# Linear attention into a two-expert router on one core: constants in pieces, gate sums moved, a new written-out order

## The chip, the core and the metric

One core of a Trainium2 chip runs the whole program. Its engines are TensorE (PE in the profile), VectorE (DVE), ScalarE (ACT), GpSimd (POOL) and SyncE (SP). Each has its own instruction queue and works through it in order; ACT, POOL and SP can also issue DMAs. The metric is the device time of one execution in microseconds (us), the median of several runs.

## The reference

```python
phi(x) = where(x > 0, x, exp(x) - 1) + 1              # on q and k
kv  = einsum('bhsd,bhse->bhde', phi(k), v);  z = sum(phi(k), axis=seq)
x   = (phi(q) @ kv) / (phi(q) . z + 1e-6)             # 8 batches, 8 heads, 576 rows of 64
x   = x as 4608 tokens of 512
noisy = x @ w_gate + log1p(exp(x @ w_noise)) * noise  # 8 experts
top2  = the two largest;  top2_w = exp(top2_l - max) / (sum + 1e-9)
out[token] = sum over its two experts e: top2_w * (relu(x @ w1[e]) @ w2[e])   # 512 -> 1024 -> 512
```

## The kernel before

**Attention.** Two batches form a group; there are four groups (0 to 3). q, k and v are loaded by POOL DMAs that turn fp32 into bf16. ACT takes the exponential of k and q (line 178), DVE makes phi of it (lines 187 and 190). PE multiplies k by v (line 210), transposes (229, 256) and makes numerators, denominators and router logits in one matmul group, `num` (line 272); DVE divides (287, 294).

**Routing.** A unit is a group, or the first six or last three of the nine column tiles of group 3 (units 3 and 4). `route(u)` is a generator of some 25 small DVE steps with a few on ACT and PE. It finds the two experts of each token (the lower-numbered is the first visit, the other the second) and each visit's rank in its expert's list. `dispatch` scatters 128 rows at a time from the tile `xr` into the DRAM table `x_sorted`, by indirect DMAs on POOL: 72 in all. A row is 512 bf16 values and four 4-byte fields (token, two gates, rank). In before.py the gates are normalised in `route` and the ranks are copied into a tile `posi`, from which the scatter takes its addresses.

**Experts.** `mm1` (line 669) and `mm2` (line 684) work on blocks of up to 512 rows. Blocks 0a, 0b, 1a, ... are named by expert; "0b" is the second block of expert 0. The first blocks hold first visits alone. A block in round 1 (0b, 1a, 2a) may be loaded when the first visits of units 0 and 1 are scattered, one in round 2 (0c, 1b, 2b, 3a) when those of unit 2 are too, and 0d when all five units are. `xt` is a transposed load, `xn` a plain one that PE transposes; both are issued on SP. Fields of a block are loaded apart, as `meta`. `mm2` also scales its result by the gate on DVE, and `put` writes it to `part` (first visits) or `out`.

**What sets the order.** Up to the end of the early blocks the order is written out by hand in `SCRIPT`: a list of words, each a call, which gives every engine its instructions in that order. `l` loads, `e`, `r`, `m` make phi, `K V T t U u Q q N n` are the attention, `R.u` is one step of `route(u)`, `D.u.s.c` scatters column tile c of unit u (s is 0 for first visits, 1 for second), `W.e.i` loads a weight matrix of expert e, `X`, `M`, `G`, `H`, `Y` are a block's load, fields, transposition, mm1 slice and mm2 tile. Behind SCRIPT, loops go over the remaining blocks (`PLAN`), unchanged here. Software DMAs of POOL use eight semaphores in turn, so that one waits until the eighth before it has landed.

Of the kernel before, what the change touches and what calls it, by code (L numbers as in the profile page):

```python
# [49 lines left out]
def build_constants(tc, consts, w_gate, w_noise, noise):  # L50
    nc = tc.nc
    c = {}
    tile_ = lambda name, shape, dt=FP32: consts.tile(shape, dt, name=name)


    wst = tile_("wst", [P, 4, 16])
    for half in range(2):
        for i, w in enumerate((w_gate, w_noise)):
            nc.scalar.dma_start(
                out=wst[64 * half : 64 * half + 64, :, 8 * i : 8 * i + 8],  # L60
                in_=w[256 * half : 256 * half + 256, :].rearrange("(a p) e -> p a e", p=64),
            )
    noise_sb = c["noise"] = tile_("noise_sb", [P, 4, 9, E])
    for g in range(4):
        nc.scalar.dma_start(
            out=noise_sb[:, g], in_=noise[g * 2 * S : (g + 1) * 2 * S, :].rearrange("(p c) e -> p c e", c=9))

    ident = c["ident"] = tile_("ident", [P, P], BF16)
    nc.gpsimd.memset(ident[:], 0.0)
    nc.gpsimd.affine_select(  # L70
        out=ident[:], in_=ident[:], compare_op=ALU.not_equal, fill=1.0,
        base=0, pattern=[[-1, P]], channel_multiplier=1,
    )
    c["gap"] = tile_("gap", [P, 8])
    ut = c["ut"] = tile_("ut", [P, P], BF16)
    nc.gpsimd.memset(ut[:], 0.0)
    nc.gpsimd.affine_select(
        out=ut[:], in_=ut[:], compare_op=ALU.is_ge, fill=1.0,
        base=0, pattern=[[-1, P]], channel_multiplier=1,
    )  # L80
    iota = lambda t, pattern, base, mult: nc.gpsimd.iota(
        t, pattern=pattern, base=base, channel_multiplier=mult, allow_small_or_imprecise_dtypes=True)

    tokid = c["tokid"] = tile_("tokid", [P, 9])
    iota(tokid[:], [[1, 9]], 0, 9)
    rowpos = c["rowpos"] = tile_("rowpos", [P, T_CAP])
    iota(rowpos[:], [[P, T_CAP]], 0, 1)

    c8 = c["c8"] = tile_("c8", [P, E])
    iota(c8[:], [[-1, E]], E, 0)  # L90
    nc.vector.tensor_scalar(out=c8[:], in0=c8[:], scalar1=1.0 / E, scalar2=None, op0=ALU.mult)

    ones = c["ones"] = tile_("ones", [P, P], BF16)
    nc.vector.memset(ones[:], 1.0)  # L94
    carry = c["carry"] = tile_("carry", [P, 2 * E])
    iota(carry[:], [[REGION, 2 * E]], 0, 0)
    c["bound"] = [tile_(f"bound{i}", [P, EARLY]) for i in range(len(ROUNDS))]
    for t, (_, q) in zip(c["bound"], ROUNDS):
        for e in range(EARLY):
            nc.vector.memset(t[:, e : e + 1], float(e * REGION + q[e]))  # L100
    rank0 = c["rank0"] = tile_("rank0", [P, 2 * E])
    iota(rank0[:], [[REGION, 2 * E]], 0, 0)

    c["f0"], c["s0"] = tile_("f0", [P, E]), tile_("s0", [P, E])
    for t, n, base in ((c["f0"], N_F, 0), (c["s0"], N_S, E * REGION)):
        step = n[1] - n[0]
        iota(t[:, 0:4], [[REGION + step * P, 4]], base + n[0] * P, 0)
        iota(t[:, 4:E], [[REGION + step * P, 4]], base + 4 * REGION + n[4] * P, 0)
    c["wst"], c["wblk"] = wst, tile_("wblk", [P, 4, 32], BF16)
    return c  # L110


class PhaseA:


    def __init__(self, rows, attn, rout, tc, q, k, v, x_sorted, psum):
# [14 lines left out]
        self.x, self.e, self.kvps, self.pqt, self.qtp, self.rden, self.r, self.ps, self.posi = {}, {}, {}, {}, {}, {}, {}, {}, {}  # L131

    def buffers(self):

        self.nc.vector.memset(self.v[:, 8:12, :], 1.0)
        self.xr = [self.pers.tile([P, 9, ROW_W], BF16, name=f"xr{i}") for i in range(3)]
        self.lwt = self.pers.tile([P, 9, 8, 16], FP32, name="lwt")
        self.kvbd = [self.kvp.tile([P, 2, 4, KVW], BF16, name=f"kvbd{i}") for i in range(2)]
        for t in self.kvbd:
            self.nc.vector.memset(t[0:64, :, :, 65:130], 0.0)  # L140
            self.nc.vector.memset(t[64:P, :, :, 0:65], 0.0)
        for t in self.xr:
            self.nc.vector.memset(t[:, :, HD:ROW_W], 0.0)
# [157 lines left out]
    def route(self, u):  # L301
# [72 lines left out]
        nc.vector.tensor_reduce(out=rank, in_=pr, op=ALU.add, axis=AX.X)  # L374
        yield
# [3 lines left out]
        yield  # L379
        nc.vector.scalar_tensor_tensor(out=gr, in0=ge[:, 0], scalar=1e-9, in1=ge[:, 1], op0=ALU.add, op1=ALU.add)  # L380
        yield
        nc.vector.reciprocal(out=gr, in_=gr)
        yield
        for i in range(2):
            tt(fld(1 + i), ge[:, i], gr, ALU.mult)
# [698 lines left out]
```

## Time and profile before

| | us |
|---|---|
| median of 3 runs (lowest to highest) | 415.59 (415.16 to 416.53) |
| the profiled execution | 419.67 |
| its span, first to last instruction | 417.9 |
| PE busy | 344.8 (83%) |
| POOL busy | 269.6 (65%) |
| ACT busy, DVE busy | 181.1, 178.1 |

The profile is of one execution, a little slower than the median. A busy PE is not a PE at its peak; what matters is where PE is idle, and what ends that. The page also gives the share of time in which the 16 DMA engines were busy; it can be over 1, since packets overlap.

### The profile page before, as it was taken

How to read it: one execution, taken by the hardware profiler on the slowest of the kernel's cores; microseconds unless marked ns; L12 is line 12 of the kernel's file. 1: busy time of each engine (PE TensorE's matmuls, PEld its weight loads, DVE VectorE, ACT ScalarE, POOL GpSimd, SP SyncE). 2: the span in 40 equal slices, each digit the busy share in tenths (PEclk: the TensorE clock that was granted, in tenths of full speed). 3: DMA queues.
4: the chain of work that ended last, by engine and by line, in shares of the span. 5: the costliest groups of instructions: out<-in, count | busy, mean ns of one | idle time of the engine just before them, and what ended most of it. 6: DMA issues, size and time to landing. Idle time of an engine off the chain costs nothing.

```text
span 417.9 us, 6947 instructions
## 1 busy us (share of the span) xinstructions
PE 344.8 (83%) x2519; PEld 205.5 (49%) x2549; DVE 178.1 (43%) x452; ACT 181.1 (43%) x342; POOL 269.6 (65%) x405
## 2 busy tenths in 40 slices
PE   0985666555751999989999999999999999999990
PEld 0354555444531665745556555644544544564440
DVE  0845979897770665113242324312421322332130
ACT  1569375754430443535444443443334334325410
POOL 8450158888768266875207576869849867898761
PEclk9996756888695899999999999999999999999997
DMA  8999999999999959998858999999997999954551
GB/s 123 205 207 207 234 199 220 216 196 174 208 215 194 244 175 271 228 252 271 149 164 180 181 243 212 205 261 192 303 249 161 245 145 312 214 181 130 172 200 57
DMA packets 83441, 85.59 MB, mean 205 GB/s; under 512 B 42911, under 2 KB 66146, under 8 KB 83398
## 3 DMA queue, kind: packets, MB, share of 16 engines
q0 software_dynamic: 36416, 63.92, 72.0%
q1 hardware_dynamic: 39222, 20.86, 23.1%
q10 hardware_dynamic: 7760, 0.28, 1.8%
q8 instruction: 22, 0.36, 0.3%
q14 instruction: 21, 0.17, 0.1%
HBM read 77.13 MB, written 33.79 MB: 265 GB/s over the span
## 4 chain that ended last, share of the span: by engine, by line
PE 66%; DMA 14%; POOL 7%; DVE 6%; issue 3%; ACT 3%; POOLq 0%; SPq 0%; DVEq 0%
PE b L669 29%; PE b L684 28%; DMA w<-in_moe_w_dram 6%; POOL x_sorted L412 4%; DMA xt<-x_sorted 3%; PE num L149 3%; DMA xn<-x_sorted 3%; DMA x_sorted<-xr,posi 2%; PE b L210 2%; DVE e L190 2%; PE num L272 2%; ACT e L178 2%; POOL kq L164 1%; DVE xr L287 1%; PE t L615 1%
## 5 line engine op out<-in xcount | busy, mean ns | idle before, releaser
L671 ACT ACTIVATE hT<-b 128x256 bf16<-128x256 f32 (+5 forms) x224 | 101.3, 460 | 153.9 <-PE b L669 147.6
L669 PE MATMUL b<-xt,w 128*128 128x256 bf16 (+5 forms) x890 | 149.0, 315 | 17.9 <-DMA xt<-x_sorted 16.7
L684 PE MATMUL b<-w,hT 128*128 128x512 bf16 (+1 forms) x616 | 141.9, 380 | 1.3
L669 PEld LDWEIGHTS <-w 128*128 128x128 bf16 x896 | 86.4, 99 | 72.4 <-issue 11.0
L412 POOL DMA_INDIRECT x_sorted<-xr,posi x72 | 75.9, 1054 | 30.9 <-issue 14.5
L684 PEld LDWEIGHTS <-hT 128*128 128x128 bf16 (+1 forms) x640 | 59.1, 99 | 63.2 <-issue 1.9
L178 ACT ACTIVATE e<-kq 128x2304 bf16<-128x2304 bf16 x16 | 33.4, 2127 | 23.3 <-DMA kq<-in_k_dram 12.8
L706 POOL DMA_INDIRECT out_dram<-y,si x34 | 33.7, 991 | 9.4 <-issue 5.5
L651 POOL DMA_INDIRECT L<-part,gi x34 | 34.8, 1023 | 7.7 <-issue 7.7
L651 POOL DMA_INDIRECT L<-part,mgi x12 | 12.0, 1003 | 37.9 <-issue 26.9
L272 PE MATMUL num<-kvbd,pqt 128*64 128x162 bf16 x288 | 18.4, 298 | 11.4 <-DVE xr L287 7.5
L287 DVE TENSOR_TENSOR xr<-num,rden 128x768 bf16<-128x768 f32 x24 | 22.7, 950 | 0.2
L272 PEld LDWEIGHTS <-pqt 128*64 128x64 bf16 x288 | 15.0, 145 | 14.5 <-DVE xr L287 8.4
L688 DVE SCALAR_TENSOR_TENSOR y<-b,mgate,L 128x512 f32<-128x512 f32 (+1 forms) x12 | 9.0, 746 | 30.8 <-PE b L684 23.9
L190 DVE TENSOR_TENSOR e<-e,kq 128x2304 bf16<-128x2304 bf16 x16 | 21.2, 1348 | 0.1
L149 PE MATMUL num<-ones 128*128 128x512 bf16 x44 | 12.2, 449 | 10.9 <-DVE ones L94 10.9
L210 PE MATMUL b<-v,e 64*128 64x192 bf16 x144 | 17.4, 289 | 2.8 <-DVE e L190 2.8
L164 POOL DMA_DIRECT2D v<-in_v_dram x20 | 13.6, 701 | 7.9 <-DMA kq<-in_q_dram 3.2
L164 POOL DMA_DIRECT2D kq<-in_k_dram x10 | 6.6, 694 | 17.3 <-DVE rden L281 12.4
L688 DVE SCALAR_TENSOR_TENSOR y<-b,meta7S,L 128x512 f32<-128x512 f32 (+1 forms) x10 | 7.5, 750 | 23.5 <-PE b L684 17.4
L210 PEld LDWEIGHTS <-e 64*128 64x128 bf16 x288 | 14.9, 113 | 5.1 <-DVE e L190 3.7
L210 PE MATMUL misc<-v,e 64*128 64x192 bf16 x144 | 17.4, 289 | 0.0
(165 smaller groups left out, 345.9 us busy)
## 6 DMA issues: line engine op xcount, KB each, us to landing
w<-in_moe_w_dram POOLq DMA_DIRECT2D x16, 1024.0 KB, 10.9
part<-y SPq DMA_DIRECT2D x39, 256.0 KB, 5.7
kq<-in_k_dram POOLq DMA_DIRECT2D x6, 576.0 KB, 9.8
kq<-in_q_dram POOLq DMA_DIRECT2D x6, 576.0 KB, 7.8
v<-in_v_dram POOLq DMA_DIRECT2D x12, 288.0 KB, 13.3
v<-in_v_dram POOLq DMA_DIRECT2D x8, 144.0 KB, 9.0
kq<-in_k_dram POOLq DMA_DIRECT2D x4, 288.0 KB, 7.5
kq<-in_q_dram POOLq DMA_DIRECT2D x4, 288.0 KB, 10.6
```

Of the source, the lines that this page charges most:

```text
L149: self.nc.tensor.matmul(out=ps[:, i % 4, 0:512], lhsT=self.c["ones"][:], rhs=_ap(self.c["ones"], [[0, 4], [1, P]]), start=True, stop=True)
L178: self.nc.scalar.activation(out=e, in_=x, func=ACT.Exp)
L190: nc.vector.tensor_tensor(out=e, in0=e, in1=x, op=ALU.min)
L210: nc.tensor.matmul(out=self.kvps[g, h, j][:, KVM * i : KVM * i + KVM], lhsT=e[half, hp, ci, :], rhs=v[half, hp + 8 - step : hp + 9 + step ...
L272: self.nc.tensor.matmul(out=ps[half, hp, KVW * i : KVW * i + KVW], lhsT=self.pqt[g, 3 * t + i][:, hp, half], rhs=self.kvbd[g % 2][:, j, hp ...
L287: nc.vector.tensor_tensor(out=_ap(xr, [[64, 4], [ROW_W, 3], [1, 64]], off=3 * t * ROW_W + 256 * s), in0=_ap(ps, [[512, 4], [KVW, 3], [1, 6 ...
L412: r = self.nc.gpsimd.indirect_dma_start(out=self.x_sorted, out_offset=bass.IndirectOffsetOnAxis(ap=self.posi[u][:, ci, sl : sl + 1], axis= ...
L651: r = nc.gpsimd.indirect_dma_start(out=L[0:m].bitcast(INT32), out_offset=None, in_=self.part.bitcast(INT32), in_offset=bass.IndirectOffset ...
L669: nc.tensor.matmul(out=ps[:, 0:n], lhsT=w1[:, dc, fc * P : fc * P + P], rhs=b["xt"][:, dc, 0:n], start=(dc == 0), stop=(dc == 3))
L671: nc.scalar.activation(out=b["hT"][:, fc, 0:n], in_=ps[:, 0:n], func=ACT.Relu)
L684: nc.tensor.matmul(out=ps[i * m : i * m + m], lhsT=b["hT"][:, f, t * P : t * P + m], rhs=w2[:, f, :], start=(fc == 0), stop=(fc == 8 // n ...
L706: r = nc.gpsimd.indirect_dma_start(out=self.out, out_offset=bass.IndirectOffsetOnAxis(ap=self.m[e, kind, i]["si"][0:m], axis=0), in_=y[0:m ...
```

## The change

Constants are built in pieces, as words of SCRIPT: `ones` and the warm-up matmuls (52 for 44) come first on DVE and PE, the router weights are loaded on SP and the noise on ACT between its exponentials (both were on ACT ahead of all else). Group 0 loads k, then v, then q (v came first). `route` writes exponentials and ranks straight into the scattered row; the scatter takes its addresses from there. The division by the gates' sum is done by `gates`, three DVE instructions for a `meta` tile before its first use. `mm2` is split: its evacuation and `put` are a word of their own, `y`. And SCRIPT is in a new order.

```diff
-        posi = self.posi[u] = self.rt.tile([P, 9, 2], INT32, name="posi", bufs=len(UNITS))
-        nc.vector.tensor_copy(out=_ap(posi, [[1, 2], [2, n]]), in_=rank)
-        nc.vector.tensor_copy(out=fld(3).bitcast(INT32), in_=rank[:, 0])
-        nc.vector.scalar_tensor_tensor(out=gr, in0=ge[:, 0], scalar=1e-9, in1=ge[:, 1], op0=ALU.add, op1=ALU.add)
-        nc.vector.reciprocal(out=gr, in_=gr)
-        for i in range(2):
-            tt(fld(1 + i), ge[:, i], gr, ALU.mult)
+        nc.vector.tensor_reduce(out=pair(3).bitcast(INT32), in_=pr, op=ALU.add, axis=AX.X)
...
-            out_offset=bass.IndirectOffsetOnAxis(ap=self.posi[u][:, ci, sl : sl + 1], axis=0),
+            out_offset=bass.IndirectOffsetOnAxis(ap=row[:, HD // 2 + 3 + sl : HD // 2 + 4 + sl], axis=0),
...
+    def gates(self, f):
+        nc, n = self.nc, f.shape[1]
+        d = self.mp.tile([P, T_CAP], FP32, name="gsum")[:, 0:n]
+        nc.vector.scalar_tensor_tensor(out=d, in0=f[:, :, 1], scalar=1e-9, in1=f[:, :, 2], op0=ALU.add, op1=ALU.add)
+        nc.vector.reciprocal(out=d, in_=d)
+        nc.vector.tensor_tensor(out=f[:, :, 1:3], in0=f[:, :, 1:3], in1=_ap(d, [[1, n], [0, 2]]), op=ALU.mult)
...
 SCRIPT = """
-l.v0.0 l.k0.0 l.k0.1 l.q0.0 l.q0.1 C l.v0.1 l.k1 e.k0.1 e.k0.0 r.k0.1 m.k0.1 r.k0.0 m.k0.0 l.q1 l.v1 e.q0.0 e.q0.1 wb
+l.k0.0 buf.1 c.ones warm.52 l.k0.1 buf.2 e.k0.0 l.v0.0 l.q0.1 c.squares l.q0.0 r.k0.0 c.counts l.v0.1 l.k1 c.router
```

Up to the last first visit of units 0 and 1, POOL has 29 scatters and four weight loads before, and 27 scatters and four weight loads now; W.1.0 has moved ahead of five scatters of unit 0, and W.2.0, which stood two places behind that last first visit, stands nine scatters behind it.

Three places show what moves. SP, from the zeros to the first results: `meta0F` and the first `xt` are of block 0a, the next `xt` of 0b, 1a and 2a. Before and after:

```order
L807 DMA part<-zrow 1x288
L466 DMA meta0F_914<-x_sorted 128x2x4
L589 DMA_TRANSPOSE xt<-x_sorted 128x4x256 x2
L589 DMA_TRANSPOSE xt<-x_sorted 128x4x384
L589 DMA_TRANSPOSE xt<-x_sorted 128x4x256
L466 DMA meta1F_1708<-x_sorted 128x3x4
```
```order
L836 DMA part<-zrow 1x288
L466 DMA meta0F_918<-x_sorted 128x2x4
L610 DMA_TRANSPOSE xt<-x_sorted 128x4x256
L466 DMA meta2F_1691<-x_sorted 128x2x4
L610 DMA_TRANSPOSE xt<-x_sorted 128x4x256
L610 DMA_TRANSPOSE xt<-x_sorted 128x4x384
```

The fields of 2a now stand ahead of the rows of 0b. PE, from the second `num` of group 3 (hT is 0a's, w_834 and w_839 are expert 0's w2, w_833 and w_838 its w1), before and after:

```order
L272 MATMUL num<-kvbd_187,pqt 64x162
L684 LDWEIGHTS hT
L684 MATMUL b<-w_834,hT 128x512
...
L669 LDWEIGHTS w_833
L669 MATMUL b<-xt,w_833 128x256
```
```order
L277 MATMUL num<-kvbd_115,pqt 64x162
L690 LDWEIGHTS w_838
L690 MATMUL b<-xt,w_838 128x256
...
L704 LDWEIGHTS hT
L704 MATMUL b<-w_839,hT 128x512
```

One slice of 0b (H.0b.7, which needs its `xt`) now stands ahead of the first mm2 tile of 0a (Y.0a.0). POOL, at the first scatter of unit 3 (xr_184 and xr_179 hold unit 2, xr_182 and xr_177 unit 3), before and after:

```order
L412 DMA x_sorted<-xr_184,posi 73984x288
L405 MEMSET gap 128x8
L412 DMA x_sorted<-xr_182,posi 73984x288
L405 MEMSET gap 128x8
L412 DMA x_sorted<-xr_184,posi 73984x288
```
```order
L412 DMA x_sorted<-xr_177 73984x288
L404 MEMSET gap 128x8
L412 DMA x_sorted<-xr_179 73984x288
L404 MEMSET gap 128x8
L412 DMA x_sorted<-xr_179 73984x288
L404 MEMSET gap 128x8
L412 DMA x_sorted<-xr_179 73984x288
```

Before, all first visits of unit 2 stand ahead of unit 3's first scatter (the one behind it is a second visit); now three of them (D.2.0.3, D.2.0.8, D.2.0.2) stand behind D.3.0.1.

## Rows read from the trace of the kernel before

**Rows 1.** Busy time by stage (counts in brackets), then granted clock, DMA share, GB/s

```profile
23.00:44.00 21.00, 13.81 (x201) 11.49 (x202) 12.23 (x17) 15.62 (x20) 5.30 (x9) 0.74 1.21 208
...
120.00:133.50 13.50, 2.82 (x31) 1.55 (x32) 5.53 (x16) 0.85 (x2) 11.55 (x21) 0.70 1.09 182
133.50:165.00 31.50, 30.80 (x206) 18.86 (x210) 19.37 (x79) 11.52 (x33) 16.52 (x30) 0.91 0.96 227
165.00:188.50 23.50, 21.30 (x160) 14.73 (x160) 3.00 (x4) 12.17 (x29) 18.50 (x34) 1.00 1.03 240
188.50:240.00 51.50, 51.18 (x333) 29.48 (x337) 17.71 (x60) 24.56 (x52) 20.70 (x30) 1.00 0.84 187
...
360.00:408.00 48.00, 47.20 (x257) 23.90 (x260) 14.62 (x22) 15.22 (x33) 37.86 (x45) 1.00 0.56 175
```

**Rows 2.** Chain that ended last, 113 to 190 us: start, us, what

```profile
113.83 6.61 DMA x_sorted<-xr,posi
120.46 13.03 DMA xt<-x_sorted
...
133.53 1.05 PE b L669 x4
...
173.97 2.81 DMA x_sorted<-xr,posi
...
177.05 10.86 DMA xn<-x_sorted
...
188.57 1.30 PE b L669 x8
```

**Rows 3.** DMA issues: count, KB each as written, median us to landing

```profile
w<-in_moe_w_dram POOLq DMA_DIRECT2D x16, 1024.0 KB, 10.9
...
x_sorted<-zrow SPq DMA_DIRECT2D x6, 144.0 KB, 6.9
```

**Rows 4.** Busy time in stretches of 4 us, columns as in rows 1

```profile
80.00:84.00 4.00, 3.55 (x40) 2.80 (x41) 2.66 (x12) 3.60 (x9) 3.46 (x6) 0.62 0.81 116
...
88.00:92.00 4.00, 0.60 (x8) 0.43 (x7) 3.96 (x9) 3.04 (x2) 3.70 (x4) 0.90 0.78 226
...
104.00:108.00 4.00, 1.16 (x8) 0.66 (x10) 2.81 (x5) 0.11 (x1) 3.04 (x5) 0.61 0.77 148
```

**Rows 5.** Timeline of the start: start, us, what [idle before <-releaser]

```profile
10.87 12.24 PE L149 MATMUL num<-ones 128*128 128x512 bf16 x44 [10.87 <-DVE ones L94]
...
14.86 8.16 ACT L178 ACTIVATE e<-kq 128x2304 bf16<-128x2304 bf16 x4 [12.83 <-DMA kq<-in_k_dram]
```

**Rows 6.** Timeline of PE, 100 to 170 us

```profile
121.37 1.90 PE L684 MATMUL b<-w,hT 128*128 128x512 bf16 x7
...
136.84 1.83 PE L272 MATMUL num<-kvbd,pqt 128*64 128x162 bf16 x24
...
164.00 0.60 PE L669 MATMUL b<-xt,w 128*128 128x256 bf16 x4
```

**Rows 7.** Timeline of POOL

```profile
118.65 0.81 POOL L459 DMA_DIRECT2D w<-in_moe_w_dram  x1 [2.40 <-PE misc L256]
...
148.58 1.00 POOL L412 DMA_INDIRECT x_sorted<-xr,posi  x1 [9.31 <-ACT hT L671]
...
149.88 0.97 POOL L412 DMA_INDIRECT x_sorted<-xr,posi  x1 [0.18 <-issue]
```

**Rows 8.** Timeline of SP, the load of block 0c

```profile
152.93 1.24 SPq L589 DMA_TRANSPOSE xt<-x_sorted  x1
```

**Rows 9.** Timeline of DVE, end of a route step chain (unit 0)

```profile
60.96 0.30 DVE L374 TENSOR_REDUCE rank<-pr 128x18 f32<-128x144 f32 x1
...
62.06 0.30 DVE L388 TENSOR_REDUCE tot<-b 128x16 f32<-128x144 f32 x1
```

**Rows 10.** The tile xt: all its loads

```profile
DMA to landing us min/median/max: 3.8/7.6/14.6
```

More of the change, by code (lines that the diff above doesn't have):

```diff
@@ L47, in _ap @@
     return bass.AP(tensor=a.tensor, offset=a.offset + off, ap=[a.ap[0]] + dims)
[L50 to L61, printed above, removed]
-            )
[L63 to L110, printed above, removed]
@@ new lines, with __init__, tile, iota @@
+class Constants:
+    def __init__(self, tc, consts, w_gate, w_noise, noise):
+        self.nc, self.consts, self.c = tc.nc, consts, {}
+        self.w_gate, self.w_noise, self.noise = w_gate, w_noise, noise
+    def tile(self, name, shape, dt=FP32):
+        self.c[name] = self.consts.tile(shape, dt, name=name)
+        return self.c[name]
+    def iota(self, t, pattern, base, mult):
+        self.nc.gpsimd.iota(t, pattern=pattern, base=base, channel_multiplier=mult, allow_small_or_imprecise_dtypes=True)
+    def ones(self):
+        self.nc.vector.memset(self.tile("ones", [P, P], BF16)[:], 1.0)
+    def router(self):
+        wst = self.tile("wst", [P, 4, 16])
+        self.tile("wblk", [P, 4, 32], BF16)
+        for half in range(2):
+            for i, w in enumerate((self.w_gate, self.w_noise)):
+                self.nc.sync.dma_start(
+                    out=wst[64 * half : 64 * half + 64, :, 8 * i : 8 * i + 8],
+                    in_=w[256 * half : 256 * half + 256, :].rearrange("(a p) e -> p a e", p=64),
+                )
+    def noises(self, g):
+        if not g:
+            self.tile("noise", [P, 4, 9, E])
+        self.nc.scalar.dma_start(
+            out=self.c["noise"][:, g],
+            in_=self.noise[g * 2 * S : (g + 1) * 2 * S, :].rearrange("(p c) e -> p c e", c=9))
+    def squares(self):
+        nc = self.nc
+        for name, op in (("ident", ALU.not_equal), ("ut", ALU.is_ge)):
+            t = self.tile(name, [P, P], BF16)
+            nc.gpsimd.memset(t[:], 0.0)
+            nc.gpsimd.affine_select(
+                out=t[:], in_=t[:], compare_op=op, fill=1.0, base=0, pattern=[[-1, P]], channel_multiplier=1,
+            )
+        self.tile("gap", [P, 8])
+    def counts(self):
+        iota, tile_ = self.iota, self.tile
+        iota(tile_("tokid", [P, 9])[:], [[1, 9]], 0, 9)
+        iota(tile_("rowpos", [P, T_CAP])[:], [[P, T_CAP]], 0, 1)
+        iota(tile_("c8", [P, E])[:], [[-1, E]], E, 0)
+        iota(tile_("carry", [P, 2 * E])[:], [[REGION, 2 * E]], 0, 0)
+        iota(tile_("rank0", [P, 2 * E])[:], [[REGION, 2 * E]], 0, 0)
+        for t, n, base in ((tile_("f0", [P, E]), N_F, 0), (tile_("s0", [P, E]), N_S, E * REGION)):
+            step = n[1] - n[0]
+            iota(t[:, 0:4], [[REGION + step * P, 4]], base + n[0] * P, 0)
+            iota(t[:, 4:E], [[REGION + step * P, 4]], base + 4 * REGION + n[4] * P, 0)
+    def bounds(self):
+        nc, c8 = self.nc, self.c["c8"]
+        nc.vector.tensor_scalar(out=c8[:], in0=c8[:], scalar1=1.0 / E, scalar2=None, op0=ALU.mult)
+        self.c["bound"] = [self.consts.tile([P, EARLY], FP32, name=f"bound{i}") for i in range(len(ROUNDS))]
+        for t, (_, q) in zip(self.c["bound"], ROUNDS):
+            for e in range(EARLY):
+                nc.vector.memset(t[:, e : e + 1], float(e * REGION + q[e]))
@@ L130, in __init__, with buffers @@
         self.pq = pool("A_pq", 5)
[L131 to L143, printed above, removed]
+        self.x, self.e, self.kvps, self.pqt, self.qtp, self.rden, self.r, self.ps = {}, {}, {}, {}, {}, {}, {}, {}
+    def buffers(self, i):
+        if i == 0:
+            self.nc.vector.memset(self.v[:, 8:12, :], 1.0)
+        elif i == 1:
+            self.kvbd = [self.kvp.tile([P, 2, 4, KVW], BF16, name=f"kvbd{i}") for i in range(2)]
+            for t in self.kvbd:
+                self.nc.vector.memset(t[0:64, :, :, 65:130], 0.0)
+                self.nc.vector.memset(t[64:P, :, :, 0:65], 0.0)
+        else:
+            self.xr = [self.pers.tile([P, 9, ROW_W], BF16, name=f"xr{i}") for i in range(3)]
+            self.lwt = self.pers.tile([P, 9, 8, 16], FP32, name="lwt")
+            for t in self.xr:
+                self.nc.vector.memset(t[:, :, HD:ROW_W], 0.0)
     def warm(self, n):
@@ L373, in route @@
         yield
[L374 to L385 removed]
+        with nc.allow_low_precision(reason="one whole number and seven zeros are added"):
+            nc.vector.tensor_reduce(out=pair(3).bitcast(INT32), in_=pr, op=ALU.add, axis=AX.X)
         yield
@@ L685, in mm2, with mm2_ev @@
                                  start=(fc == 0), stop=(fc == 8 // n - 1), skip_group_check=n > 1)
+        b["ps", t] = ps
+    def mm2_ev(self, b, t):
+        nc, e, m, ps = self.nc, b["e"], self.rows(b, t), b["ps", t]
+        n = P // m
+        gate = self.gate(e, *b["tiles"][t])[0:m]
         y = b["y", t] = self.rot(self.yp, "yy").tile([P, HD], FP32, name="y")
@@ L935, in do_Y, with do_y @@
         self.pb.mm2(self.blocks[k], int(t))
+    def do_y(self, k, t):
+        self.pb.mm2_ev(self.blocks[k], int(t))
         self.pb.put(self.blocks[k], int(t))
```

108 lines of the change are left out of this document (65 added, 43 removed).

## The prediction, on record before the result

> **What bounds the kernel now.** I read the busy time by stage first [rows 1]. From 188.5 us on PE is busy 51.18 of 51.5 us, and at the end still 47.20 of 48, at full clock. The loops there are unchanged, so the change can only move the moment at which PE gets there. From 133.5 to 188.5 PE is nearly full too (30.80 of 31.5 and 21.30 of 23.5 us); before 133.5 it is mostly waiting, 10.7 of the last 13.5 us.
>
> The chain that ended last [rows 2] tells what PE waits for. At 113.83 POOL issues the last first visit of unit 1; it lands 6.61 us later, at 120.46; only then may SP issue the rows of block 0b, which take 13.03 us, and at 133.53 PE starts on them. A second such chain ends at 187.95: the last first visit of unit 4 is issued at 173.97, the rows of 0d are issued at 177.05 and take 10.86 us. PE is at that point 2 us early (the idle rest of 165 to 188.5 [rows 1]).
>
> Under the first chain lies the DMA engines' capacity. Between 23 and 44 us they move 208 GB/s at a share of 1.21 [rows 1], with ACT and DVE far from full; I take that as their limit in this stage. By 120.46 they have moved q, k and v (8 x 8 x 576 x 64 values of 2 bytes are 4,608 KB each), four weight halves of 1,024 KB, six zero blocks of 144 KB [rows 3] and 29 scatters of 128 rows of 1,152 bytes, 144 KB each: 13,824 + 4,096 + 864 + 4,176 = 22,960 KB, 23.5 MB. At 208 GB/s that is 113 us; with some 3 us until the first bytes move and 1.3 us for 0a's 256 KB, 117 of the 120.46. The front is a transfer that is never far from its limit; its slack is in a few dips, of which I see three, with shares of 0.81, 0.78 and 0.77 [rows 4]: against 1.21 they lose (0.40 + 0.43 + 0.44) x 4 / 1.21 = 4.2 us.
>
> **The change, part by part.**
> *Start.* PE's 44 warm-ups hold it from 10.87 to 23.11 and the first exponential waits for k until 14.86 [rows 5]. With k ahead of v's 576 KB, k is there 576 KB / 208 GB/s = 2.8 us sooner; the warm-ups start before POOL's constants, and eight more of them cost 8 x 12.24 / 44 = 2.2 us that PE has. But v's second half and q are behind the same sum of bytes, so the attention of group 0 gains 1 to 3 us at its first numerators, and by the argument above the scatters cannot land sooner than their bytes. I count this as what lets the dips be filled, not as a term of its own; without that cover its worth is at most the 2.8 us.
>
> The eight constant loads leave ACT's head, where ACT waits for k anyway, and go to SP (idle) and, four of them, between exponentials, on an ACT busy 15.62 of 21 us [rows 1] whose work the scatters' bytes hide: zero; without that cover four issues as long as the other queue's 1.24 us [rows 8] at most, 5 us.
>
> *Issue of 0b.* Two scatters fewer stand ahead: 288 KB, 1.4 us. Of the dips' 4.2 us I take half, 2.1 (bounds 0 and 4.2): work starts sooner at their left, but they come where POOL itself is dense. 2a's fields are issued ahead of 0b's rows: 0.5 us, bounds 0 and 1.24 (SP's issue of another load [rows 8]). 120.46 - 1.4 - 2.1 + 0.5 = 117.5.
>
> *Transfer of 0b.* Before, the load of W.2.0 (1,024 KB) is issued at 118.65 [rows 7] and shares the engines with it. Now W.2.0 stands nine scatters later. All xt loads range from 3.8 to 14.6 us, median 7.6 [rows 10]; scatters still go on, so I take 10.0 between 7.6 and 13.03. Rows of 0b at 127.5, 6.0 us sooner.
>
> *Y.0a.0 behind H.0b.7.* Before, this tile ran at 121.37, in the wait (7 recorded matmuls in 1.90 us [rows 6]). Now it runs behind the wait, at a clock that has fallen (0.70 granted over the stretch [rows 1], so near 1.2 GHz at its end): twice that, up to 4.3 us for eight, say 3.0. Behind it stand N.3.2 on PE, and by it the steps of route unit 3 on DVE and ACT. Before, N.3.2 ended 5.1 us behind 0b's landing (136.84 + 1.83 [rows 6] - 133.53), three 0b slices and N.3.2 all at a low clock. Now it is one slice (1.05 [rows 2]), the tile (3.0), two slices and N.3.2 at a clock that has meanwhile risen, about half of 2 x 1.05 and two thirds of 1.83: 6.3 to 6.5, so +1.4 us for unit 3. Against it, the gate sum and the copies leave the chain between rank and `tot`: 61.26 to 62.06, 0.8 us [rows 9]. Net +0.6 (bounds -0.8 and +3.4). Unit 3's first scatter: 148.58 [rows 7] - 6.0 + 0.6 = 143.2. POOL waited 9.31 us for it before and will again.
>
> *Scatters up to 0d.* From unit 3's first scatter to the last first visit stood 17 scatters and a weight load behind the first one; now it is 19. Two more at 1.30 us (148.58 to 149.88 [rows 7]): +2.6. 0d's rows land at 187.91 - 6.0 + 0.6 + 2.6 = 185.1.
>
> *Blocks of round 2.* D.2.0.2 now stands fourth from unit 3's first scatter: 143.2 + 3 x 1.30 = 147.1, landing 6.6 us later (as at 113.83 [rows 2]; bound below 2.81, as at 173.97) at 153.7. SP then issues 3a's and 0c's rows, 1.24 us, and 0c takes the median 7.6 us: 162.5, and 1b another 0.5: 163.0. Before, 0c was issued at 152.93 [rows 8] and PE came to it at 164.00 [rows 6], unhindered. Now PE comes to it at 127.5 + 30.5 (133.5 to 164.0) + 3.0 = 161.0 and waits for 2 us. This stall is new; it takes the place of part of what 0b's wait gave back.
>
> *End of SCRIPT.* From 164.00 to PE's wait at 185.95 are 21.95 us of work; two slices of 3a (8 matmuls 1.30 us [rows 2]) have moved ahead of 0d's transposition: 163.0 + 21.95 + 1.3 = 186.25, later than 0d's rows (185.1), so no wait. Behind it 1.3 us less is left: 187.95 - 186.25 + 1.3 = 3.0 us gained.
>
> *Gates in the expert stage.* Three small DVE instructions for each field tile, none over 0.3 us; DVE is busy 17.71 of 51.5 us there [rows 1] and PE has several result buffers. Zero; without that cover some 0.6 us for each of about 20 tiles.
>
> Sum: 417.9 - 3.0 = 414.9 of span. The profiled execution, 419.67, stands 4.1 over the median of 415.59; I take the 3.0 from the median: 412.6.
>
> **The rivals.**
> *The front gives no more than its bytes* (slower). If DMA is at its limit all the way, 0b is issued at 120.46 - 1.4 + 0.5 = 119.6, and if scatters slow it as W.2.0 did, it lands at 132.6. The price is then decided by POOL's order: D.2.0.2 issues at 152.2 and lands at 158.8, 0c and 1b are there at 168.1, and PE gets to 0d's transposition at 168.1 + 21.95 + 1.3 = 191.35, 3.4 us later than before, with 1.3 us less behind it: 2.1 us slower, 417.7. It decides from a landing of 0b at about 130.5 on. For it speaks the sum of bytes; against it the three dips. The Trainium skill is on this rival's side: its page "DMA: Bandwidth & Descriptors", section "Issuing engines are not separate DMA queues", says that DMAs started by several engines run on the same 16 DMA engines and interleave, so that more queues save only the time to issue. By that rule the front's length is the bytes', and the time 417.7; the share of 1.21 agrees, the dips do not.
> *The dips close and 0b's transfer is quick.* All 4.2 us and 7.6 us of transfer: 0b at 123.0, 4.5 us sooner than forecast: 408.1. For it: an earlier attention feeds POOL in the dips, and the median transfer. Against: POOL is dense with scatters there.
> *Nothing shows.* 0b 3 us sooner, and Y.0a.0, two more scatters and the late 0c take it back: 130.5 for 0b, 415.6.
>
> **How the numbers follow.** Forecast 0.45, within 409.5 to 415; the quick front 0.17 (406.5 to 409.5); nothing 0.13; slower 0.25 (416.8 to 420). What can be told from no change is 0.3%, 414.3 to 416.8. Of the forecast's 0.45 some 0.41 is below 414.3: faster 0.58, same 0.17, slower 0.25. The range 407.0 to 418.5 leaves out about 0.08 at each end.
>
> **What would show it.** The first exponential at 10 to 12 us; the first scatter of unit 0 one to three us before 64; DMA share without dips under 0.8 between 80 and 108; 0b's rows landing at 125 to 130 and PE idle until then; unit 3's first scatter at about 143 behind an idle POOL; a PE wait of some 2 us for 0c or 1b near 161; no wait at 0d's transposition; from there the same busy PE to the end. The prediction is wrong if 0b lands after 130.5, if route unit 3 takes over 18 us from there, or if the early expert loops, come sooner, wait for second visits or weights.

## The result, and the profile after

The changed kernel takes 404.05 us in the median of four runs (403.84 to 405.32), the kernel before 415.38 beside it (415.01 to 416.53): a ratio of 0.9729, 95% interval 0.9701 to 0.9757. The forecast was 412.6 with a range from 407.0 to 418.5: the direction is right, the size is not, 11.3 us gained instead of 3.0. The profiled execution of before stands 4 us above its median, so that the two profiles lie 15.8 us apart (spans of 417.9 and 402.1), more than the medians.

The busy time by stage of the changed kernel, columns as in [rows 1] (the stage and its length, then the busy us of PE, PE's weight loads, DVE, ACT and POOL, then granted clock, DMA share and GB/s):

```profile
23.00:44.00 21.00, 11.19 (x181) 9.38 (x177) 13.89 (x20) 17.06 (x18) 5.72 (x9) 0.79 1.21 206
...
80.00:100.00 20.00, 13.90 (x206) 11.39 (x203) 16.81 (x44) 13.18 (x20) 14.79 (x23) 0.75 1.18 246
...
120.00:133.50 13.50, 12.36 (x100) 7.57 (x100) 12.64 (x47) 6.67 (x19) 8.66 (x17) 1.00 1.09 236
133.50:165.00 31.50, 31.29 (x214) 20.24 (x217) 13.43 (x52) 14.15 (x36) 26.14 (x47) 1.00 1.02 259
165.00:188.50 23.50, 22.56 (x145) 12.89 (x146) 6.72 (x38) 11.89 (x24) 15.27 (x27) 1.00 0.87 250
188.50:240.00 51.50, 51.24 (x342) 30.22 (x346) 20.40 (x60) 22.21 (x52) 25.12 (x34) 1.00 0.95 195
```

The stretch to look at is 120 to 133.5 us: PE is busy for 12.36 of 13.5 us, where [rows 1] had 2.82, and the granted clock is 1.00 instead of 0.70. From 188.5 on PE is as full as before (51.24 of 51.5 us, against 51.18). The chain that ended last, 95 to 180 us (start, us, what), answers to [rows 2]:

```profile
95.18 10.33 DMA xt<-x_sorted
105.64 3.57 PE b L690 x16
...
119.45 0.60 PE b L690 x4
...
159.43 4.87 DMA x_sorted<-xr
164.41 9.60 DMA xn<-x_sorted
174.06 0.62 PE t L636 x8
```

The load of 0b's rows is no longer in it; the first load in it is that of 0a's rows. The timeline of PE shows the same (answers to [rows 6]; 0b's first slice is at 119.44, Y.0a.0 at 119.88, N.3.2 at 123.21, the slices of 0c begin at 150.22):

```profile
105.64 3.57 PE L690 MATMUL b<-xt,w 128*128 128x256 bf16 x16 [5.22 <-DMA xt<-x_sorted]
...
119.44 0.61 PE L690 MATMUL b<-xt,w 128*128 128x256 bf16 x4
119.88 1.89 PE L704 MATMUL b<-w,hT 128*128 128x512 bf16 x7
...
123.21 1.04 PE L277 MATMUL num<-kvbd,pqt 128*64 128x162 bf16 x24
...
150.22 5.40 PE L690 MATMUL b<-xt,w 128*128 128x256 bf16 x48
...
174.06 0.62 PE L636 MATMUL t<-ident,xn 128*128 128x128 bf16 x8 [0.83 <-DMA xn<-x_sorted]
```

Neither 0b nor 0c is waited for. PE comes to the first slice of 0b 14.1 us sooner than in the profile before (119.44 against 133.53), to 0c 13.8 us sooner (150.22 against 164.00) and to 0d's transposition 13.9 us sooner (174.06 against 187.95): nearly all of the 15.8 us between the two profiles are won by the time 0b starts.

The timeline of POOL, with the last first visit of unit 1 (108.57), W.2.0 (121.44) and unit 3's first scatter (133.29), answers to [rows 7]:

```profile
108.57 0.97 POOL L412 DMA_INDIRECT x_sorted<-xr  x1 [0.18 <-issue]
...
121.44 0.83 POOL L459 DMA_DIRECT2D w<-in_moe_w_dram  x1
...
133.29 1.00 POOL L412 DMA_INDIRECT x_sorted<-xr  x1 [3.48 <-ACT hT L692]
```

The timeline of SP, with the rows of 0b, 1a and 2a in one merged line from 115.02 and those of 0c at 142.08 [rows 8]:

```profile
115.02 5.18 SPq L610 DMA_TRANSPOSE xt<-x_sorted  x3
...
142.08 1.29 SPq L610 DMA_TRANSPOSE xt<-x_sorted  x1
```

0b's rows were issued at 115.02 and PE used them at 119.44 without a wait: at most 4.4 us under way, where [rows 2] had 13.03. The start, in the timeline of ACT, answers to [rows 5]:

```profile
7.76 2.12 ACT L183 ACTIVATE e<-kq 128x2304 bf16<-128x2304 bf16 x1 [5.73 <-DMA kq<-in_k_dram]
```

### The profile page after: what moved, and what is told of

Its sections match the earlier page's. It is cut to its first block, busy times and chain, and to the rows that moved or that the text cites. A ratio compares the mean times of both kernels' runs of the same rounds, so it can differ in the third digit from the quotient of the medians.

```text
span 402.1 us, 7018 instructions
## 1 busy us (share of the span) xinstructions
PE 344.0 (86%) x2527; PEld 204.8 (51%) x2557; DVE 186.1 (46%) x506; ACT 181.6 (45%) x342; POOL 267.4 (67%) x405
## 4 chain that ended last, share of the span: by engine, by line
PE 61%; DMA 20%; POOL 7%; DVE 5%; issue 3%; ACT 2%; POOLq 0%; SPq 0%; DVEq 0%
PE b L690 30%; PE b L704 29%; DMA kq<-in_k_dram 7%; POOL x_sorted L412 4%; DMA x_sorted<-xr 3%; DMA xt<-x_sorted 3%; DMA xn<-x_sorted 2%; DMA w<-in_moe_w_dram 2%; DMA kq<-in_q_dram 2%; DVE e L195 1%; DVE xr L292 1%; ACT e L183 1%; PE t L636 1%; DVE kq L192 1%; POOL kq L169 1%
## 5 line engine op out<-in xcount | busy, mean ns | idle before, releaser
L690 PE MATMUL b<-xt,w 128*128 128x256 bf16 (+5 forms) x890 | 147.5, 313 | 6.7 <-DMA xt<-x_sorted 5.2
L412 POOL DMA_INDIRECT x_sorted<-xr x72 | 74.6, 1036 | 28.5 <-issue 12.5
L672 POOL DMA_INDIRECT L<-part,gi x34 | 34.8, 1024 | 7.9 <-issue 7.9
L277 PE MATMUL num<-kvbd,pqt 128*64 128x162 bf16 x288 | 17.0, 282 | 12.5 <-DVE xr L292 10.1
L277 PEld LDWEIGHTS <-pqt 128*64 128x64 bf16 x288 | 13.8, 136 | 15.0 <-DVE xr L292 10.9
L169 POOL DMA_DIRECT2D v<-in_v_dram x20 | 12.4, 636 | 10.1 <-DMA v<-in_v_dram 3.6
L541 POOL DMA_INDIRECT xm<-x_sorted,m_idx x12 | 12.2, 1018 | 8.0 <-DMA x_sorted<-xr 5.1
L739 POOL MEMSET gap<- 128x416 f32 x36 | 16.8, 468 | 0.0
```

What stands on the lines that cost most here:

```text
L277: self.nc.tensor.matmul(out=ps[half, hp, KVW * i : KVW * i + KVW], lhsT=self.pqt[g, 3 * t + i][:, hp, half], rhs=self.kvbd[g % 2][:, j, hp ...
L412: r = self.nc.gpsimd.indirect_dma_start(out=self.x_sorted, out_offset=bass.IndirectOffsetOnAxis(ap=row[:, HD // 2 + 3 + sl : HD // 2 + 4 + ...
L672: r = nc.gpsimd.indirect_dma_start(out=L[0:m].bitcast(INT32), out_offset=None, in_=self.part.bitcast(INT32), in_offset=bass.IndirectOffset ...
L690: nc.tensor.matmul(out=ps[:, 0:n], lhsT=w1[:, dc, fc * P : fc * P + P], rhs=b["xt"][:, dc, 0:n], start=(dc == 0), stop=(dc == 3))
L739: nc.gpsimd.memset(self.c["gap2"][:], 0.0)
```

## The experiments

**The chips.** The five sets of experiments ran on four chips, and these are of two kinds. On two (three sets) the kernel before takes 416.6 to 416.7 us; on the other two (the first and the last set) it takes 436.5 to 437.9. There the profile has waits that end on nothing recorded, "remote" and "issue", on ACT, DVE and PE. These are waits of the kernel before on such a chip, 100 to 200 us (total, times, longest):

```profile
ACT hT L671 <- remote: 14.5, 7, 5.3
...
ACT kvbd L222 <- issue: 5.7, 1, 5.7
```

The first profile of before has no "remote" wait, and no "issue" wait of ACT. I call these chips the ones with pauses, and draw conclusions on the changed kernel only from the others; each ratio is to the kernel before on the same chip.

**The kernel before, profiled again** (`before_again`, a chip with pauses):

> The kernel before, unchanged, profiled a second time: its first profiled execution stood 4 us above its median. If the slow transfer of 0b's rows belongs to the kernel (the load of W.2.0 stands right ahead of it), the rows take 11 to 14 us again and the excess of 4 us lies elsewhere. If it belonged to that one execution, they take under 9 us, 0b starts before 129, and the time is about 415.

436.46 us, one run. 0b's rows are issued at 118.67, and PE starts on them at 128.34 behind a wait of 1.2 us: 9.7 us, between the two expectations. The wait is short because PE itself comes later there (Y.0a.0 at 125.25, against 121.37). It does not settle whether the 13 us belong to the kernel; `code_only_b` below, on the other kind of chip, shows nearly as much.

**The changed kernel as yardstick** (`after_again`, `after_third`, `after_fourth`, chips without pauses):

> The changed kernel unchanged, beside the ones below, since the chip of the first four experiments showed pauses of several us on ACT, DVE and PE that the first two profiles do not have. If the gain belongs to the kernel, the ratio is 0.97 again within 0.01, with 0b's rows there before PE comes to them. If it belonged to the first chip, the ratio is above 0.985.

> The changed kernel unchanged, as the yardstick for the three below on their chip: a ratio to before of 0.97 to 0.98, 0b's rows there without a long wait, and between 0 and 4 us of waiting for the rows of 0c and 1b near 152.

> The changed kernel unchanged, as the yardstick on this chip: a ratio to before of 0.973 to 0.98, 0a's rows 8 to 11 us under way, PE waiting 4 to 6 us for them.

408.86, 406.68 and 408.68 us: ratios of 0.9797 (0.9724 to 0.9870), 0.9789 (0.9739 to 0.9839) and 0.9778 (0.9704 to 0.9853). So the gain belongs to the kernel on such chips, and is nearer to 2.1% than to the 2.7% of the first comparison. The rows of 0c and 1b were waited for in one of the three profiles, `after_again` (timeline of PE):

```profile
151.68 0.60 PE L690 MATMUL b<-xt,w 128*128 128x256 bf16 x4 [2.29 <-DMA xt<-x_sorted]
153.95 4.30 PE L690 MATMUL b<-xt,w 128*128 128x256 bf16 x23 [1.67 <-DMA xt<-x_sorted]
```

**W.2.0 back in the way** (`w2_early`, with pauses; `w2_early_b`, without):

```diff
-D.1.0.4 D.1.1.3
+D.1.0.4 W.2.0 D.1.1.3
...
-D.2.1.0 D.2.0.0 W.2.0 D.2.0.5
+D.2.1.0 D.2.0.0 D.2.0.5
```

> The changed kernel with one word moved: the load of W.2.0 (1,024 KB) right behind the last first visit of unit 1, as before, instead of nine scatters later. If the weight load in the way of 0b's rows was the main cost, these take over 9 us instead of under 5, PE waits for them again, and the time is 408 to 412. If the front is simply sooner and the weight load is no hindrance, they stay under 6 us and the time within 1 us of 404.

> The changed kernel with W.2.0 right behind the last first visit of unit 1, once more, now to be read against the changed kernel on the same chip. If the weight load in the way of 0b's rows is the main part, it gives back 5 to 9 us of the changed kernel's gain, and PE waits for 0b's rows. If it only looked so, less than 2 us.

With pauses 442.25 us, a ratio of 1.0126 (1.0068 to 1.0184). Without: 413.75 us, 0.9949 (0.9908 to 0.9990), 4.9 us above the changed kernel by the medians, 6.3 by the ratios ((0.9949 - 0.9797) x 416.7). The timeline of PE in `w2_early_b`:

```profile
118.80 1.04 PE L277 MATMUL num<-kvbd,pqt 128*64 128x162 bf16 x24 [1.78 <-DVE xr L292]
124.57 1.03 PE L690 MATMUL b<-xt,w 128*128 128x256 bf16 x4 [4.74 <-DMA xt<-x_sorted]
```

and of POOL and SP there, W.2.0 and the rows (the line of SP merges the issue of three lists, 0b's first):

```profile
109.54 0.83 POOL L459 DMA_DIRECT2D w<-in_moe_w_dram  x1
```

```profile
115.09 9.56 SPq L610 DMA_TRANSPOSE xt<-x_sorted  x3
```

0b's rows are issued at the same time as in the changed kernel, but take 9.5 us (115.09 to 124.57), and the wait is back: the weight load ahead of them does it.

**The kernel before with W.2.0 out of the way** (`before_w2_late`, with pauses; `before_w2_late_b`, without):

```diff
-n.3.0.2 R.2 q.3.2 W.2.0 D.1.1.3
+n.3.0.2 R.2 q.3.2 D.1.1.3
...
-D.2.0.1 D.1.1.5 D.2.0.2
+D.2.0.1 D.1.1.5 W.2.0 D.2.0.2
```

> The kernel before with one word moved: W.2.0 eight scatters later, behind the last scatter of unit 1's first visits and some of unit 2. If the weight load in the way of 0b's rows was the main cost, they take 4 to 8 us instead of 13, 0b starts 5 us sooner, and the time is 409 to 412. If not, the time is within 1 us of 415.4.

> The kernel before with only W.2.0 moved eight scatters later, once more, beside the changed kernel. If the weight load is the main part, it takes more than half of the changed kernel's gain: a ratio to before of 0.98 to 0.985. If it is a lesser part, 0.99 to 1.0.

430.25 us, 0.9853 (0.9794 to 0.9911), and 412.51 us, 0.9864 (0.9783 to 0.9946). The second is just outside both forecasts and nearer to that of a main part. Timelines of SP and PE in `before_w2_late_b`:

```profile
123.21 4.72 SPq L589 DMA_TRANSPOSE xt<-x_sorted  x3
```

```profile
127.55 0.61 PE L669 MATMUL b<-xt,w 128*128 128x256 bf16 x4 [0.57 <-DMA xt<-x_sorted]
```

One word moved in the old kernel takes 0b's rows from 13.1 to 4.3 us and gives about two thirds of the whole gain on that chip (0.0136 of 0.0203 by the ratios, each known to 0.7 or 0.8%).

**The new code in the old order** (`code_only`, with pauses; `code_only_b`, without): the changed kernel's functions, with before's SCRIPT in their words:

```diff
-l.q0.1 C l.v0.1
+l.q0.1 c.router c.noises.0 c.noises.1 c.noises.2 c.noises.3 c.squares
+c.counts c.ones c.bounds buf.0 buf.1 buf.2 warm.44 l.v0.1
...
-M.2a n.3.1.0 n.3.1.1 n.3.1.4 n.3.1.2 Y.0a.0 n.3.1.3
+M.2a n.3.1.0 n.3.1.1 n.3.1.4 n.3.1.2 Y.0a.0 y.0a.0 n.3.1.3
```

> The code of the changed kernel (gates in the expert stage, ranks into the row, constants in pieces) with the order of before: v first, all constants behind the first loads, 44 warm-ups, W.2.0 ahead of 0b, each gated eviction right behind its matmuls. If the order makes the gain, this takes 414 to 416.5. If the shorter route chains make it (some 1.5 us for each of five units), it takes 407 to 412.

> The code of the changed kernel with the order of before, once more on another chip: v first, all constants behind the first loads, W.2.0 ahead of 0b. If the order makes the gain, a ratio to before of 0.995 to 1.003. If the shorter route chains make a good part of it, 0.985 to 0.99.

438.55 us, 1.0018 (0.9978 to 1.0058), and 418.78 us, 1.0047 (1.0010 to 1.0084): the code alone gains nothing; on the second chip it costs 0.1 to 0.8%, on the first nothing clear of the noise. In `code_only_b` POOL issues W.2.0 at 116.21 and SP the rows of 0b at 118.05, and PE:

```profile
129.91 1.03 PE L690 MATMUL b<-xt,w 128*128 128x256 bf16 x4 [8.19 <-DMA xt<-x_sorted]
```

That is 11.9 us: the slow transfer of [rows 2] was no accident of one execution.

**The old start** (`start_back`): the changed kernel with the words that `code_only` has up to the zero blocks; the first of them are

```diff
-l.k0.0 buf.1 c.ones warm.52 l.k0.1 buf.2 e.k0.0 l.v0.0 l.q0.1
+l.v0.0 l.k0.0 l.k0.1 l.q0.0 l.q0.1 c.router c.noises.0 c.noises.1
```

> The changed kernel with the start of before up to the zero blocks (v first, all constants behind the first loads, 44 warm-ups), the rest as changed. If the earlier start is only a cover for the dips, as the prediction has it, this loses 0 to 3 us. If the earlier start is what lets every later load and scatter come sooner, it loses 4 to 8 us, with 0b issued 3 to 5 us later.

409.97 us, 0.9781 (0.9682 to 0.9881), no difference to the changed kernel on this chip. But 0b's rows are issued at 117.95 instead of 115.15, and PE waits for them until 121.85: the start is worth 2.8 us there, by one profile of each. Most of it is given back, since `after_again` then waits 4.0 us for 0c and 1b and not for 0d, and this kernel 2.0 us for 0d and not for 0c.

**Other weight loads moved** (`w1_late`, the first two pairs; `w0_late`, the others):

```diff
-^ X.0a W.1.1 D.1.0.8
+^ X.0a D.1.0.8
-D.2.1.1 D.2.0.7 D.2.0.6
+D.2.1.1 D.2.0.7 W.1.1 D.2.0.6
...
-D.0.0.6 D.0.1.2 W.0.1 M.0a
+D.0.0.6 D.0.1.2 M.0a
-D.1.0.0 D.1.0.5 D.1.0.6
+D.1.0.0 D.1.0.5 W.0.1 D.1.0.6
```

> The changed kernel with the load of W.1.1 (1,024 KB), which stands right ahead of the unit's scatters while 0a's rows are under way, moved behind 0b's rows. If a weight load beside a transposed load is what makes such a load take 8 to 13 us instead of 3 to 5, 0a's rows take under 6 us and PE's wait for them (4 to 5 us) nearly goes; 0b's rows are issued some 1.3 us sooner, and the time falls by 1 to 4 us. If scatters and q, k, v loads alone make it slow, 0a's rows still take 8 us or more and the time stays within 1 us.

> The changed kernel with the load of W.0.1 (1,024 KB) moved from some 6 us ahead of the issue of 0a's rows to right behind it. If a weight load slows a list of rows only when it is issued ahead of it, 0a's rows take 4 to 6 us instead of 10 and PE's wait for them falls from 5 to under 1 us; the time falls by at most 2 us, since 0b's rows then bound PE. If what slows 0a's rows is the sum of all transfers around them, they still take 8 us or more and the time stays the same.

`w1_late`: 413.54 us, 0.9931 (0.9901 to 0.9960), 6.9 us above the changed kernel by the medians, 5.9 by the ratios. 0a's rows (95.01 to 104.96) still take 10 us: this weight load is issued behind them. 0b's rows are issued 3.8 us sooner (111.93 against 115.75 in `after_third`), but three weight loads now stand close together (117.55, 122.38, 129.23), and POOL's scatters wait for them: each of the two below is the eighth POOL DMA behind a weight load, as the eight semaphores have it (135.80 behind the load at 122.38, 143.64 behind that at 129.23). Its timeline of POOL:

```profile
135.80 0.97 POOL L412 DMA_INDIRECT x_sorted<-xr  x1 [2.76 <-DMA w<-in_moe_w_dram]
...
143.64 0.96 POOL L412 DMA_INDIRECT x_sorted<-xr  x1 [1.67 <-DMA w<-in_moe_w_dram]
```

and of PE, where 0c and 1b are late:

```profile
152.55 1.01 PE L690 MATMUL b<-xt,w 128*128 128x256 bf16 x4 [3.27 <-DMA xt<-x_sorted]
154.77 3.57 PE L690 MATMUL b<-xt,w 128*128 128x256 bf16 x16 [1.21 <-DMA xt<-x_sorted]
```

`w0_late`: 411.63 us, 0.9780 (0.9697 to 0.9863), no difference. 0a's rows take 7.3 us (97.14 to 104.45) instead of 10.2 (96.12 to 106.32 in `after_fourth`), between the two expectations. But the changed kernel itself has 8.2 us in `after_again` (95.90 to 104.07), and the load that was moved is issued 0.3 us behind the rows (97.47), so that it still runs beside them. What makes 0a's rows slow stays open.

**First visits ahead** (`first_visits`: those left of units 2 to 4; `both`: with `w1_late`'s edit; `u_first`: those of units 0 and 1, with W.0.1 and W.1.0 behind 0a's rows); one piece of the first and one of the last:

```diff
-D.3.0.1 D.2.0.3 D.2.0.8 D.2.0.2 D.3.0.2 D.1.1.6 D.3.0.3 D.3.0.0 D.3.1.2
+D.3.0.1 D.3.0.2 D.3.0.3 D.3.0.0 D.3.0.4 D.3.0.5 D.1.1.2 D.2.1.4
...
-D.0.0.0 D.0.0.1 D.0.1.1 D.0.1.4 D.0.1.0 D.0.0.3 W.0.0
+D.0.0.0 D.0.0.1 D.0.0.3 D.0.0.8 D.0.0.4 D.0.0.7 W.0.0
```

> The changed kernel with the remaining first visits of units 2, 3 and 4 ahead of second visits, no weight load moved past more than one scatter. If the round-2 blocks and 0d wait for the scatters that stand last (the prediction's 2-us stall at 0c), their rows come 4 and 8 us sooner, the waits at 0c, 1b and 0d go, and the time falls by 0.8 to 4 us, as large as these waits are in the changed kernel on this chip. If something else holds them, the time stays within 0.5 us.

> Both edits, W.1.1 later and first visits ahead. If each takes away its own wait, the gains add: 2 to 7 us below the changed kernel. If what PE gains early it loses at the next list of rows, this is no better than the better of the two.

> The changed kernel with the first visits of units 0 and 1 ahead of their second visits, W.0.1 and W.1.0 behind the issue of 0a's rows. If POOL's order sets when 0a's and 0b's rows may be issued, 0a's are issued 6 to 10 us sooner and 0b's 3 to 5 us sooner, PE waits for 0a no more, comes to 0b 2 to 4 us sooner, and the time falls by 1 to 4 us. If DMA's bytes set it, the rows come no sooner or later lists (0c, 1b, 0d) take it back, and the time stays within 1 us or rises.

`first_visits`: 408.65 us, 0.9776 (0.9737 to 0.9816), the same as the changed kernel: 0d's rows are issued at 157.28 instead of 166.20 and its wait goes, but that wait was only 0.97 us there. `both`: 411.72 us, 0.9889 (0.9860 to 0.9919), between `w1_late` and `first_visits` and worse than the latter: the edits do not add. `u_first`: 411.76 us, 0.9891 (0.9828 to 0.9953), slower. Its 0a is issued at 82.87 and no longer waited for, but 0b's rows leave no sooner (116.79), behind these waits of POOL, and PE waits for them (POOL, then PE):

```profile
98.81 1.40 POOL L412 DMA_INDIRECT x_sorted<-xr  x1 [2.18 <-DMA w<-in_moe_w_dram]
...
105.49 0.94 POOL L459 DMA_DIRECT2D w<-in_moe_w_dram  x1 [2.00 <-DMA w<-in_moe_w_dram]
```

```profile
122.42 1.03 PE L690 MATMUL b<-xt,w 128*128 128x256 bf16 x4 [6.31 <-DMA xt<-x_sorted]
```

What PE gains at 0a it loses at 0b. No version beat the changed kernel.

**Start and W.2.0 together; Y.0a.0 ahead of 0b** (`start_w2`, which is `code_only` with the changed start and W.2.0 as in `before_w2_late`; `y_front`, below):

```diff
-H.0b.7 Y.0a.0 H.0b.0
+Y.0a.0 H.0b.7 H.0b.0
```

> The code of the changed kernel, its start up to the zero blocks, and from there the order of before with only W.2.0 moved eight scatters later. If these two places make the whole gain, a ratio to before of 0.975 to 0.982, with 0b's rows 3 to 5 us under way. If the rest of the new order has a share of a third or more, 0.983 to 0.99.

> The changed kernel with the tile Y.0a.0 ahead of the first slice of 0b again, as before. By the prediction's term (the tile behind the wait delays N.3.2 and unit 3 by 1.4 us) this gains 1 us or more: a ratio to before of 0.975 or less. Since 0b's rows are there when PE comes to them and the clock is up, I now expect no difference: 0.976 to 0.982.

Both ran on a chip with pauses: 437.40 us, 1.0026 (0.9972 to 1.0081), and 441.54 us, 1.0153 (1.0089 to 1.0218). There 0b's rows are under way from 114.87 in `y_front`, but PE comes to their first slice only at 131.26, behind Y.0a.0 at 129.52, and to the second at 136.01, behind a wait for ACT of 4.16 us; neither run answers its question for the other chips.

**0b's rows in all profiles on chips without pauses** (W.2.0's issue against that of the rows; start of issue on SP; PE's first slice). Where PE waited, the time between is that of the rows; where it did not, they were there sooner, and the time is an upper bound:

| kernel | weight load | rows issued | first slice | us between | PE's wait |
|---|---|---|---|---|---|
| before [rows 2, 7] | 1.8 ahead | 120.46 | 133.53 | 13.1 | 10.27 |
| `code_only_b` | 1.8 ahead | 118.05 | 129.91 | 11.9 | 8.19 |
| `w2_early_b` | 5.6 ahead | 115.09 | 124.57 | 9.5 | 4.74 |
| after | 6.4 behind | 115.02 | 119.44 | at most 4.4 | 0 |
| `after_again` | 8.0 behind | 115.15 | 118.54 | 3.4 | 0.67 |
| `after_third` | 7.3 behind | 115.75 | 121.12 | at most 5.4 | 0 |
| `after_fourth` | 6.7 behind | 115.16 | 119.81 | at most 4.7 | 0 |
| `before_w2_late_b` | 7.9 behind | 123.21 | 127.55 | 4.3 | 0.57 |
| `start_back` | 7.1 behind | 117.95 | 121.85 | 3.9 | 3.02 |
| `w0_late` | 6.9 behind | 117.59 | 121.17 | 3.6 | 3.38 |
| `first_visits` | 7.9 behind | 115.11 | 121.06 | 6.0 | 2.65 |
| `u_first` | 7.7 behind | 116.79 | 122.42 | 5.6 | 6.31 |
| `w1_late` | 5.6 behind (W.1.1) | 111.93 | 118.02 | at most 6.1 | 0 |
| `both` | 6.5 behind (W.1.1) | 111.74 | 120.05 | at most 8.3 | 0 |

The chips with pauses agree: with W.2.0 1.8 or 1.9 us ahead, 0b's rows take 9.7, 12.8 and 11.9 us there (`before_again`, `code_only`, `w2_early`; PE waited for them in all three).

## Why the prediction was wrong, by its own steps

**Transfer of 0b: the step that failed, by its size.** It named the right cause, the load of W.2.0, but let its move give back only 3.0 us (13.03 to 10.0), because scatters still go on beside the rows. They do, one each 1.27 us from 115.34 to 120.43 in the profile after, and the rows take at most 4.4 us all the same. The table separates the two: with W.2.0 up to 5.6 us ahead 9.5 to 13.1 us, with it behind 3.4 to 6.0 where PE waited for them. Between the two profiles the term was 8.6 us or more, not 3. By time it is shown from both sides: 0.0152 of the ratio when it is put back, 0.0136 when it alone is moved, of 0.0203 in all on that chip, which is 6.3 and 5.7 us.

**Start and issue of 0b: too small as well.** The first exponential came at 7.76, sooner than the 10 to 12 forecast, unit 0's first scatter at 61.94, within the forecast. The rows of 0b: forecast 117.5, measured 115.02, 5.4 us sooner than before instead of 3.0. Of the three dips [rows 4] the prediction let half close; in the profile after no stretch of 4 us from 80 to 108 is under 1.10, and a dip stands only behind them (the three places, and the new dip):

```profile
80.00:84.00 4.00, 2.96 (x35) 2.46 (x33) 3.65 (x14) 4.00 (x5) 3.24 (x6) 0.60 1.17 238
...
88.00:92.00 4.00, 1.17 (x16) 1.02 (x18) 3.92 (x5) 4.00 (x5) 2.09 (x3) 0.75 1.10 228
...
104.00:108.00 4.00, 2.36 (x12) 1.66 (x13) 3.65 (x13) 0.77 (x2) 3.44 (x7) 0.50 1.10 238
...
112.00:116.00 4.00, 3.25 (x55) 2.66 (x53) 1.44 (x6) 2.28 (x6) 3.02 (x7) 1.00 0.59 209
```

With all 4.2 us the prediction's own sum gives 115.4. That the dips set the moment is not shown: `after_again` keeps one (0.80 from 104 to 108 us) and issues the rows at 115.15. `start_back` puts 2.8 us down to the start, which the prediction counted as no term of its own. Nor is 208 GB/s a limit for the whole front: it is what the q, k and v loads move at a share of 1.21 (206 after, too), but from 80 to 100 us, with scatters and weights, 246 GB/s pass at a share of 1.18. Up to the issue of 0b's rows it is 211 GB/s on the mean, against 202 before. That the start gives 2.8 us at the end of the kernel isn't shown.

**Y.0a.0 and route unit 3.** Forecast: a cold tile, +0.6 us net from 0b to unit 3's first scatter. PE had no long wait before it, and the granted clock was 1.00 from 120 us on; N.3.2 ends 4.8 us behind the start of 0b's first slice (123.21 + 1.04 - 119.44; forecast 6.3 to 6.5, before 5.1), and unit 3's first scatter stands 13.85 us behind that start (119.44 to 133.29), against 15.05 before: -1.2. This hung on the wait for 0b that did not come.

**Blocks of round 2.** The new stall of 2 us is real but not steady: none in three profiles of the changed kernel, 2.29 + 1.67 us in the fourth. Where it is there, it takes back some 4 us of what 0b gave; that it takes back a part was forecast. In the profile after nothing is taken back: of its 14.1 us at 0b, 13.9 are left at 0d's transposition, where the forecast lost half of its 6.0.

**0d and the end.** 0d's rows were issued 12.6 us sooner (164.41), and PE waits 0.83 us for them, against 2.02; the forecast was no wait. From unit 3's first scatter to that landing it is 40.8 us, 1.4 more than before (39.3), where two more scatters were put down at 2.6. The loops behind are unchanged, as forecast.

**Gates and shorter route chains.** PE does not notice the gates: it is busy 51.24 of 51.5 us. But the code in the old order is not faster on either kind of chip, so the 0.8 us that the chain was to save does not show in the time.

**The rivals.** "The dips close and 0b's transfer is quick" was right in kind: the profile after shows both. Its 408.1 us lies 4 us above the first comparison and among the later ones (406.68 to 408.86). "The front gives no more than its bytes" fell: 0b's rows were there by 119.44, not at 132.6. The rule named beside it (the Trainium skill, "DMA: Bandwidth & Descriptors", section "Issuing engines are not separate DMA queues") says that DMAs interleave whichever engine started them, and the runs agree: with a load started by POOL ahead of it, one started by SP takes 9.5 to 13.1 us instead of some 4. But what the prediction drew from it for this kernel did not follow, since most of the gain came from the order of two transfers, not from the number of queues.

**Open.** About a third of the gain, 0.5 to 0.7% of the time, is not assigned: the start, the rest of the order, or both; `start_w2` was to tell and ran on a chip with pauses. The intervals behind this are wide, up to 0.8% to either side. On such chips the changed kernel itself was not measured; two kernels that differ from it in one word were 1.3 and 1.5% slower than before there. The move of W.2.0 alone gained 1.5% on one of them (`before_w2_late`), but together with the new code and start it gained nothing on the other (`start_w2`); no run explains that.

## What to carry to other kernels

Look at what is issued in the last microseconds ahead of the transfer that an idle engine waits for: here a 1 MB load that nobody needed yet made that transfer 5 to 9 us longer, and moving it behind the critical rows took one word. The shortest of such a transfer's rows in the profile (3.8 us [rows 10]) was here a better guide than the median (7.6) to what it takes once its neighbour is gone. But a large load moved into a place where others follow holds up the queue behind it, so follow it to the next list that is waited for.

## What the runs showed of the hardware

- 0b's transposing load of 256 rows takes 3.4 to 6.0 us beside scatters, and 9.5 to 13.1 when 1,024 KB were issued 1.8 to 5.6 us ahead of it by another engine. 0a's, with such a load 5.9 to 6.6 us ahead, takes 8.2 to 10.6 in the changed kernel's four profiles. One issued 7 us behind it (W.1.1 in the changed kernel, at 102.08) does not matter: without it 0a's rows still took 10 us.
- Large loads hold up POOL's later scatters: ahead of the eighth DMA behind a weight load POOL stood up to 4.37 us until that load was through (`both`; 2.76 in `w1_late`, 2.64 in `after_again`). The eight semaphores are this program's.
- The same program takes 416.6 us on some chips and 436.5 to 437.9 on others, whose ACT, DVE and PE stand for up to 5.7 us (in the rows above, of ACT) with nothing recorded that they wait for. Why is not known.
